# Feed-forward of the first batches in single units, engines chosen per operation by a table, and shifted ranks in a planned kernel

## The chip, the core and the metric

The kernel runs on one core of a Trainium2 chip. The core has a matrix engine (TensorE, in the profile PE, its weight loads PEld), three engines for element-wise work (VectorE or DVE, ScalarE or ACT, GpSimd or POOL), and SyncE (SP), which here only issues DMAs. Each engine runs its own list of instructions in order; they wait for each other through semaphores. Matrix products land in PSUM, of which there are eight banks of 128 x 512 float32; POOL is used in this kernel for data in SBUF only. The metric is the device time of one execution in microseconds, the median of several; less is better.

## What is computed

A recurrent state (40 x 40 per head, 4 batches x 8 heads, 768 time steps) is read and updated at each step, and its outputs pass through a feed-forward layer with a squared ReLU:

```python
for t in range(S):                         # S = 768
    y[:, :, t] = np.einsum('bhd,bhde->bhe', rt, state)
    Sa = np.einsum('bhde,bhe->bhd', state, at)
    state_decay = state * wt[:, :, None, :] - np.einsum('bhd,bhe->bhde', Sa, bt)
    state = state_decay + np.einsum('bhd,bhe->bhde', vt, kt)
...
x = y.transpose(0, 2, 1, 3).reshape(B * S, H * D)   # 3072 x 320
h = x @ w_in                                        # 320 x 2048
g = np.maximum(h, 0.0) ** 2
out = g @ w_out                                     # 2048 x 320
```

## The kernel before

Time is cut into six chunks of 128. Within a chunk the recurrence is solved with matrix products, so a chunk needs from the one before only the state at its boundary. One unit of input is a *batch* `m`: one chunk of one batch entry, all eight heads, 24 units in all (`m = 4 * chunk + entry`). Each batch is worked off in two *steps* of four heads, 48 in all (`st = 2 * m + u`).

**Preparation of a batch** (`add_prep`): SP loads six arrays of 160 KB (`W K B A V R`, L244). ACT takes the logarithm of `W` (L257), PE makes the prefix sum over time in float32 (`cs`, L263), ACT the two exponentials `GI` and `GA` (L268). `K` and `B` are multiplied by `GI` (`kb`, L279), `A`, `V`, `R` are cast to bfloat16 and `V` a second time into `EVX` (`cast`, L285 and L290). PE transposes in three groups of eight (`tGA`, `tKB`, `tRV`, all L294), and the results are copied out of PSUM as `GT` (ACT, L330), `AT` (DVE, L336), `KBT` (ACT, L342) and `RVT` (DVE, L347).

**A step** (`add_step`): eight products (`ca`, L394), masked by DVE into `CN` (L402, two operations), the triangular system solved by `P` (L411, L417), a copy `Mc` (L529), two corrections (`corr`, L426) with the difference `c1` between them (L439), and the result `Sn` (L536). `x1` (L443), `Cc` (L447) and the squares `jk`, `jm` (L451, L576) serve a check of the numbers at the end. Then `Sn` is transposed (`tb`, L463, with the state of four steps earlier, L469) and copied out (`TB`, L474), eight products `ex` (L482) are masked into `EVX` (L487, two DVE operations), and `kbm` (L498) with `z` (L505) gives the outputs and the next state, scaled on DVE into `YS` (L511) and `UZ` (L515).

**Feed-forward** (`add_ff`) is done for two batches at a time, twelve groups `h`. It waits for the `YS` of four steps. Rows of heads 6 and 7 are moved to free partitions by four small DMAs on SP (`mv`, L628). Eight groups `hp` of six products (256 columns each, L638) each fill a bank; ACT takes the ReLU (`hs`, L644), and POOL or DVE squares it (`Gt`, L649). Two halves `op` of eight products each per batch (L666) give the output, which ACT copies (`osb`, L670) and SP stores (L675). The weights come in by DMAs issued on POOL (`WIN`, L602; `WOUT`, L609).

**What sets the order.** Every operation is declared by `op(...)` with an engine, a rank (its due place, in steps), a cost, a latency, what it needs and which buffers it uses. `listed()` then plays the engines against each other in a model: at each turn it takes, for the engine that can start first, the lowest rank among the first 60 operations that could begin about then. Buffers come from rings (`RING`), PSUM banks from a pool of eight. The order in which operations are picked is the order in which they are issued, each engine in its own list. `share` puts empty operations on SP's list of the model, which stand for the time that the weights take from the DMA queues. `LATE` delays the moves and the stores in the model so that SP is not held by them.

Of the kernel before, what the change touches and what calls it, by code (L numbers as in the profile page):

```python
# [18 lines left out]
def kernel(  # L19
# [12 lines left out]
    nc = tc.nc  # L32
# [40 lines left out]
    class Op:  # L73
        __slots__ = ("name", "eng", "rank", "cost", "lat", "needs", "bufs", "mode", "fn", "end",
                     "order")
# [11 lines left out]
    def op(name, eng, rank, cost, lat, needs, bufs, fn, mode=None):  # L87
        o = Op()
        o.name, o.eng, o.rank, o.cost, o.lat, o.mode = name, eng, rank, cost, lat, mode
        o.needs, o.bufs, o.fn, o.end, o.order = list(needs), list(bufs), fn, None, len(ops)  # L90
        for b_ in o.bufs:
            b_.users.append(o)
        assert name not in ops, name
        ops[name] = o
# [24 lines left out]
    def pe(n):  # L119
        return n, n + 0.165  # L120

# [91 lines left out]

    class Batch:
# [23 lines left out]
    def add_load(m, key, rank):  # L238
# [8 lines left out]
        op(("L", m, key), "SP", rank, 0.97, 2.9, [], [o.nat[key]], go)  # L247

    def add_prep(m):
# [26 lines left out]
        def kb(u, key, j0, n):  # L276
            h = slice(2 * j0, 2 * j0 + 2 * n)
            eng = nc.vector if (m < 2 and key == "B") else nc.gpsimd
            eng.tensor_tensor(out=o.KB.tile[:, u, h, 0:D], in0=o.nat[key].tile[:, h],  # L279
                              in1=o.GI.tile[:, h], op=ALU.mult)  # L280

        def cast(key, j0, n):
            h = slice(2 * j0, 2 * j0 + 2 * n)
            if key == "X":
                nc.gpsimd.tensor_copy(  # L285
                    out=o.EVX.tile[:, j0:j0 + n, :, L:LV].rearrange("p i s e -> p (i s) e"),
                    in_=o.nat["V"].tile[:, h])
            else:
                pad = {"A": o.GA.tile[:, 1], "R": o.RV.tile[:, 0], "V": o.RV.tile[:, 1]}[key]
                nc.gpsimd.tensor_copy(out=pad[:, h, 0:D], in_=o.nat[key].tile[:, h])  # L290
# [5 lines left out]
        for p, (j0, n) in enumerate(o.parts):  # L296
# [6 lines left out]
            for u, key in enumerate("KB"):  # L303
                on = "DVE" if (m < 2 and key == "B") else "POOL"
                cost = 0.55 * f + 0.04 if on == "DVE" else 0.8 * f + 0.03
                op(("kb", m, key, p), on, sp - 2.2 + 0.1 * u, cost, cost + 0.07,
                   [("L", m, key), ("GI", m)] + cleared("KB", m), [o.nat[key], o.GI, o.KB],
                   lambda u=u, key=key, j0=j0, n=n: kb(u, key, j0, n))
            for x, (key, ring) in enumerate((("A", "GA"), ("V", "RV"), ("R", "RV"), ("X", "EVX"))):
# [4 lines left out]
                   lambda key=key, j0=j0, n=n: cast(key, j0, n))  # L314
# [14 lines left out]
            def e_gt(b1=b1, j0=j0, n=n):  # L329
                nc.scalar.activation(  # L330
                    out=o.GT.tile[:, j0:j0 + n, 1:L + 1], func=ACTF.Copy,
# [8 lines left out]
            def e_kb(b2=b2, j0=j0, n=n):  # L340
                t_ = sb(o.KBT, [128, 2, PB, L], BF16)
                nc.scalar.activation(  # L342
                    out=t_[:, :, j0:j0 + n], func=ACTF.Copy,
                    in_=bank(b2)[:, 0:2 * n * L].rearrange("p (u j t) -> p u j t", u=2, t=L))

            def e_rv(b3=b3, j0=j0, n=n):
                nc.vector.tensor_copy(  # L347
                    out=o.RVT.tile[:, :, j0:j0 + n, 0:L],
                    in_=bank(b3)[:, 0:2 * n * L].rearrange("p (u j t) -> p u j t", u=2, t=L))
# [3 lines left out]
            op(("GT", m, p), "ACT", sp - 1.8, *act(512 * f), [("tGA", m, p)] + cleared("GT", m),  # L353
               [b1, o.GT], e_gt)
# [3 lines left out]
               [o.KB, b2], t_kb, "F")  # L358
            op(("KBT", m, p), "ACT", sp - 1.1, *act(1000 * f), [("tKB", m, p)], [b2, o.KBT], e_kb)
            op(("tRV", m, p), "PE", sp - 0.6, *pe(0.45 * f),  # L360
               [("cast", m, "V", p), ("cast", m, "R", p)], [o.RV, b3], t_rv, "F")
            op(("RVT", m, p), "DVE", sp - 0.4, 0.065 + 0.535 * f, 0.145 + 0.535 * f,
               [("tRV", m, p)] + cleared("RVT", m), [b3, o.RVT], e_rv)


# [10 lines left out]
    def add_step(st):  # L376
# [65 lines left out]
        def x1():  # L442
            nc.gpsimd.tensor_tensor(out=sb(x1b[st], [128, 4, D], FP32)[:], in0=M(),  # L443
                                    in1=c1b[st].tile[:], op=ALU.add)

        def cc():
            nc.gpsimd.tensor_tensor(out=C(), in0=x1b[st].tile[:], in1=Sn(), op=ALU.add)  # L447
# [24 lines left out]
        def tb_ev():  # L472
            hi = 4 if carry else 2
            nc.vector.tensor_copy(out=sb(TB_, [128, 4, 128], BF16)[:, 0:hi], in_=tbv()[:, 0:hi])  # L474
# [46 lines left out]
        for s in range(2):  # L521
# [7 lines left out]
           lambda: nc.scalar.activation(out=M(), func=ACTF.Copy, in_=Pv()))  # L529
# [6 lines left out]
           lambda: nc.scalar.activation(out=Sn(), in_=Pv(), func=ACTF.Copy, scale=-1.0))  # L536
# [3 lines left out]
        op(("Cc", st), "POOL", st + 1.0, 0.43, 0.487, [("x1", st), ("Sn", st)],  # L540
           [x1b[st], o.EVX, Ccb[c]], cc)
# [4 lines left out]
        op(("TB", st), "DVE", st + 2.2, 0.065 + 0.00052 * n, 0.146 + 0.00052 * n, [("tb", st)],  # L546
           [tbb, TB_], tb_ev)
# [43 lines left out]
    def share(name, issue, n, each):  # L591
        for i in range(n):
            last = i == n - 1
            op(name if last else (*name, i), "SP", -5.0, each, each + 2.0 * last,
               [(*name, i - 1) if i else issue], [], lambda: None)

    def add_weights():
        for g in range(NG):
# [6 lines left out]
            op(("WINi", g), "POOL", 0.5 + 0.5 * g, 0.52 * n, 0.52 * n, [("WIN2",), GATE[g]], [], go)  # L605
            share(("WIN", g), ("WINi", g), n, 0.7)
# [3 lines left out]
        op(("WOUTi",), "POOL", 2.5, 1.23, 1.3, [GATE[3]], [], go)  # L610
        share(("WOUT",), ("WOUTi",), 9, 0.92)
        op(("WIN2",), "DVE", -5.0, 1.0, 1.1, [], [], lambda: nc.vector.memset(WIN[2][:], 0.0))

    Gtb = [buf("Gt") for _ in range(NH)]

    def add_ff(h):
        c, hf = divmod(h, 2)
        st0 = c * NQ + hf * (NQ // 2)
        done = [("YS", st0 + i) for i in range(NQ // 2)]
        X_ = YSb[c]  # L620

        def by_pair():
            return X_.tile[:].rearrange("e (b p) t -> e p b t", b=NB)[:, :, HB * hf:HB * hf + HB, :]
# [332 lines left out]
```

## Time and profile before

| what | value |
|---|---|
| time, median of three runs | 294.0 us (293.79 to 295.83) |
| the profiled execution | 294.21 us, its span 292.5 us |
| mean granted clock of TensorE | 0.967 |
| instructions | 9938 |
| data read and written in HBM | 28.84 and 3.93 MB |

The profile is of one execution. Its span is what the trace covers, 1.7 us less than that execution's time. Busy time is the union of an engine's instructions; the instructions of one engine overlap at their ends, so two that follow each other start closer together than the mean duration of one. The chain of waits, followed back from the last instruction, lies on PE for most of its length:

```profile
## 4 chain that ended last, share of the span: by engine, by line
PE 72%; DVE 9%; POOL 7%; ACT 6%; issue 2%; DMA 1%; POOLq 0%; DVEq 0%; ACTq 0%
```

Ends and starts that are used below: PE's first prefix sum starts at 4.43 us, its last product ends at 286.6 us; the last `osb` starts at 286.60 us.

### The profile page before, as it was taken

To read this page: it belongs to the slowest core of one execution; us is meant where nothing else is said; L and a number is where in the kernel's file an instruction comes from. 1 tells how busy PE (TensorE), PEld (TensorE's weight loads), DVE (VectorE), ACT (ScalarE), POOL (GpSimd) and SP (SyncE) were. 2 spreads that over 40 slices of the span, in tenths; PEclk is the share of its full clock that TensorE was granted. 3 is DMA by queue.
4 is the path that set the end of the run, shared out by engine and by line. 5 is a ranking of instruction groups with operands and counts; after the bars stand their busy time and mean duration, and the time that the engine had idled before them with its cause. 6 is when DMAs were issued, how large, how long until landed. Compare 5 with 4: busy or idle time off the path is not lost.

```text
span 292.5 us, 9938 instructions
## 1 busy us (share of the span) xinstructions
PE 272.7 (93%) x3852; PEld 216.1 (74%) x3852; DVE 227.7 (78%) x523; ACT 201.2 (69%) x531; POOL 202.9 (69%) x350
## 2 busy tenths in 40 slices
PE   6897879799998999999999999999999999999991
PEld 4665647487776788878788888888888888777871
DVE  7869988537699999999987987987987887771120
ACT  3657565387978689687687696796695776644641
POOL 7799654659998849887867878868868556555400
PEclk9959789799999999999999999999999999999998
DMA  7999794599999596978959958920010010001111
GB/s 135 180 175 183 122 174 80 102 175 180 170 173 165 101 175 120 163 136 139 192 98 178 172 101 152 145 53 25 2 31 22 2 31 25 10 23 33 44 48 53
DMA packets 158472, 31.37 MB, mean 107 GB/s; under 512 B 152976, under 2 KB 158096, under 8 KB 158416
## 3 DMA queue, kind: packets, MB, share of 16 engines
q1 hardware_dynamic: 155808, 28.03, 53.8%
q0 software_dynamic: 2608, 2.62, 5.7%
q8 instruction: 32, 0.52, 0.8%
q14 instruction: 24, 0.20, 0.2%
HBM read 28.84 MB, written 3.93 MB: 112 GB/s over the span
## 4 chain that ended last, share of the span: by engine, by line
PE 72%; DVE 9%; POOL 7%; ACT 6%; issue 2%; DMA 1%; POOLq 0%; DVEq 0%; ACTq 0%
PE bank L638 20%; PE bank L666 17%; PE bank L294 9%; PE bank L498 5%; PE bank L263 4%; PE bank L394 4%; PE bank L426 3%; PE bank L482 3%; DVE EVX L487 3%; DVE CN L402 3%; PE bank L505 2%; POOL KB L279 2%; PE bank L463 2%; ACT jk L451 2%; PE bank L469 1%
## 5 line engine op out<-in xcount | busy, mean ns | idle before, releaser
L649 POOL TENSOR_TENSOR Gt<-hs 128x512 bf16<-128x512 bf16 x66 | 68.6, 1043 | 23.0 <-ACT hs L644 22.0
L638 PE MATMUL bank<-YS,WIN 120*128 120x256 bf16 (+1 forms) x576 | 77.0, 273 | 0.0
L487 DVE TENSOR_TENSOR EVX<-bank,MEX 128x512 bf16<-128x512 f32 x96 | 64.9, 683 | 11.4 <-PE bank L482 9.2
L644 ACT ACTIVATE hs<-bank 128x512 bf16<-128x512 f32 x96 | 57.5, 601 | 22.5 <-PE bank L638 20.0
L402 DVE TENSOR_TENSOR CN<-bank,MCN 128x512 bf16<-128x512 f32 x96 | 64.5, 679 | 1.1 <-PE bank L394 1.1
L666 PE MATMUL bank<-WOUT,Gt 128*128 128x320 bf16 x384 | 60.2, 301 | 0.3 <-ACT GA L268 0.2
L638 PEld LDWEIGHTS <-WIN 120*128 120x128 bf16 (+1 forms) x576 | 51.8, 97 | 9.9 <-issue 0.6
L451 ACT ACTIVATE jk<-CN 128x512 bf16<-128x512 bf16 x48 | 30.3, 631 | 23.5 <-DVE CN L402 23.4
L666 PEld LDWEIGHTS <-Gt 128*128 128x128 bf16 x384 | 36.0, 98 | 13.5 <-issue 0.5
L443 POOL TENSOR_TENSOR x<-Mc,c 128x160 f32<-128x160 bf16 x48 | 23.5, 490 | 22.5 <-DVE c L439 21.9
L342 ACT ACTIVATE KBT<-bank 128x1024 bf16<-128x1024 bf16 (+1 forms) x25 | 24.7, 988 | 6.9 <-PE bank L294 6.8
L649 DVE TENSOR_TENSOR Gt<-hs 128x512 bf16<-128x512 bf16 x30 | 14.2, 473 | 19.6 <-ACT hs L644 19.3
L426 PEld LDWEIGHTS <-CN 128*128 128x128 bf16 x384 | 21.5, 98 | 10.3 <-issue 4.9
L279 POOL TENSOR_TENSOR KB<-NK,GI 128x320 bf16<-128x320 f32 (+1 forms) x25 | 21.2, 846 | 9.6 <-ACT GI L268 9.1
L447 POOL TENSOR_TENSOR Cc<-x,EVX 128x160 bf16<-128x160 f32 x48 | 23.7, 493 | 5.7 <-ACT EVX L536 4.9
L498 PE MATMUL bank<-EVX,KB 128*64 128x168 bf16 x384 | 23.7, 243 | 1.6 <-DVE EVX L487 1.6
L474 DVE COPY TB<-bank 128x512 bf16<-128x512 bf16 (+1 forms) x48 | 18.6, 393 | 3.7 <-PE bank L469 1.8
L511 DVE TENSOR_TENSOR YS<-bank,GT 128x256 bf16<-128x256 f32 x48 | 20.2, 420 | 1.1 <-PE bank L505 0.6
L439 DVE TENSOR_TENSOR c<-bank,Mc 128x160 bf16<-128x160 f32 x48 | 15.1, 317 | 7.3 <-PE bank L426 7.1
L394 PE MATMUL bank<-AT,KBT 64*128 64x128 bf16 x384 | 19.6, 226 | 1.2 <-DVE AT L336 1.1
L515 DVE TENSOR_TENSOR UZ<-bank,GT 64x80 bf16<-64x80 f32 x80 | 18.8, 235 | 1.9 <-PE bank L498 0.8
L263 PE MATMUL bank<-lnW,UTI 128*128 128x320 f32 x48 | 19.6, 491 | 0.8 <-DVE EVX L487 0.4
(82 smaller groups left out, 535.1 us busy)
## 6 DMA issues: line engine op xcount, KB each, us to landing
NW<-in_w_dram SPq DMA_DIRECT2D x24, 160.0 KB
NK<-in_k_dram SPq DMA_DIRECT2D x24, 160.0 KB
NB<-in_b_dram SPq DMA_DIRECT2D x24, 160.0 KB
NA<-in_a_dram SPq DMA_DIRECT2D x24, 160.0 KB
NV<-in_v_dram SPq DMA_DIRECT2D x24, 160.0 KB
NR<-in_r_dram SPq DMA_DIRECT2D x24, 160.0 KB
out_dram<-osb SPq DMA_DIRECT2D x24, 160.0 KB
WOUT<-in_moe_w_out_dram POOLq DMA_DIRECT2D x1, 1280.0 KB, 10.6
```

Of the source, the lines that this page charges most:

```text
L263: nc.tensor.matmul(out=csb.tile[:, 0:NHH * D], lhsT=UTI[:], rhs=o.lnW.tile[:], start=True, stop=True)
L279: eng.tensor_tensor(out=o.KB.tile[:, u, h, 0:D], in0=o.nat[key].tile[:, h], in1=o.GI.tile[:, h], op=ALU.mult)
L394: nc.tensor.matmul(out=quads(ca[s])[:, i, u, :], lhsT=o.KBT.tile[half(s), u, j0 + i, :], rhs=o.AT.tile[half(s), j0 + i, :], start=(i == 0 ...
L402: nc.vector.tensor_tensor(out=t_[:, :, s], in0=quads(ca[s]), in1=MCN[:], op=ALU.mult)
L426: nc.tensor.matmul(out=P[:, 2 * i + s], lhsT=CN[:, i, s, 1, :], rhs=X[:, 2 * i + s], start=False, stop=last, skip_group_check=True)
L451: nc.scalar.activation(out=t_[:], in_=CN_.tile[:, :, :, 1, :], func=ACTF.Square, accum_out=ACC[:, AN + st:AN + st + 1])
L487: nc.vector.tensor_tensor(out=EVX[:, :, s, 0:2 * LV].rearrange("p i (u x) -> p i u x", u=2)[:, :, :, 0:L], in0=quads(ex[s]), op=ALU.mult, ...
L498: nc.tensor.matmul(out=uy()[half(s), i, :], lhsT=o.KB.tile[:, u, 2 * (j0 + i) + s, :], rhs=EVX[:, i, s, LV * u:LV * u + LV], start=(i == 0 ...
L638: nc.tensor.matmul(out=hp[:, u], lhsT=WIN[g][0:ROWS[g], j * 128:(j + 1) * 128], rhs=by_pair()[0:ROWS[g], g], start=(g == 0 and u == 0), st ...
L644: nc.scalar.activation(out=sb(hsb, [128, 512], BF16)[:], in_=hpb.tile[:], func=ACTF.Relu)
L649: eng.tensor_tensor(out=t_[:, 2 * jj:2 * jj + 2].rearrange("p j a b -> p (j a b)"), in0=hsb.tile[:], in1=hsb.tile[:], op=ALU.mult)
L666: nc.tensor.matmul(out=opb.tile[:, 0:DM], lhsT=Gtb[h].tile[:, j, b_, :], rhs=WOUT[:, j, :], start=(j == 0), stop=(j == NJ - 1))
```

## The change

1. The feed-forward of batches 0 to 3 is done for one batch at a time, in groups of twelve products of 128 columns; from batch 4 on it stays with pairs. There are fourteen groups `h` instead of twelve. Their ranks follow the last step of the unit.
2. Many operations get a list of other engines on which they could run (`alts`): `kb` POOL or DVE, `cast` POOL, DVE or ACT, `GT`, `KBT`, `RVT`, `TB`, `Mc`, `Sn`, `hs` and `osb` ACT or DVE, `x1` and `Cc` POOL or DVE, the squares `Gt` any of the three. A string of digits, `WAYS`, names the one taken for each.
3. A second string, `MOVES`, shifts the rank of every operation, in tenths of a step.
4. The model has two DMA queues (`h` for those issued on SP, `s` for POOL) in place of the empty operations of `share`, and PE is 1.4 times slower in it before 56 us. The transposes name the buffers into which their results are copied, so that the plan reserves these earlier.

```diff
-    def op(name, eng, rank, cost, lat, needs, bufs, fn, mode=None):
+    def op(name, eng, rank, cost, lat, needs, bufs, fn, mode=None, alts=()):
+        o.alts = [(eng, cost, lat), *alts] if alts else []
+        o.fn = (lambda: fn(o.eng)) if alts else fn
...
+    def copy(eng, out, in_, scale=None):
+        if eng == "ACT":
+            nc.scalar.activation(out=out, in_=in_, func=ACTF.Copy,
+                                 **({} if scale is None else {"scale": scale}))
+        elif scale is None:
+            (nc.gpsimd if eng == "POOL" else nc.vector).tensor_copy(out=out, in_=in_)
+        else:
+            nc.vector.tensor_scalar(out=out, in0=in_, scalar1=scale, scalar2=None, op0=ALU.mult)
+    def engine(eng):
+        return nc.gpsimd if eng == "POOL" else nc.vector
...
-        op(("L", m, key), "SP", rank, 0.97, 2.9, [], [o.nat[key]], go)
+        op(("L", m, key), "SP", rank, 0.78, 0.78, [], [o.nat[key]], go)
+        ops["L", m, key].dma = "h", 0.85
...
-                   lambda key=key, j0=j0, n=n: cast(key, j0, n))
+                   lambda eng, key=key, j0=j0, n=n: cast(key, j0, n, eng),
+                   alts=[("DVE", *vec(320 * f)), ("ACT", *act(320 * f))])
...
-               [o.GA, b1], t_ga, "F")
+               [o.GA, b1, o.GT, o.AT], t_ga, "F")
...
-        op(("x1", st), "POOL", st + 0.9, 0.43, 0.487, [("c1", st)], [Mcb[c], c1b[st], x1b[st]], x1)
+        op(("x1", st), "POOL", st + 0.9, 0.43, 0.487, [("c1", st)], [Mcb[c], c1b[st], x1b[st]], x1,
+           alts=[("DVE", *vec(160))])
...
-    Gtb = [buf("Gt") for _ in range(NH)]
+    FFS = [(0,), (1,), (2,), (3,)] + [(m, m + 1) for m in range(4, NBC, 2)]
+    Gtb = [buf("Gt") for _ in FFS]
     def add_ff(h):
-        c, hf = divmod(h, 2)
-        st0 = c * NQ + hf * (NQ // 2)
-        done = [("YS", st0 + i) for i in range(NQ // 2)]
+        ms = FFS[h]
+        c, b0 = divmod(ms[0], NB)
+        nb, last = len(ms), 2 * ms[-1] + 1
+        NU = 4 // nb
+        done = [("YS", 2 * m + i) for m in ms for i in range(2)]
...
-            op(("mv", h, x), "SP", st0 - 9.0 + 0.01 * x, 0.82, 2.0, done, [X_], gather)
-        for jj in range(NJ // 2):
+            op(("mv", h, x), "SP", last - 12.0 + 0.01 * x, 0.75, 0.75, done, [X_], gather)
+            ops["mv", h, x].dma = "h", 0.1
+        for jj in range(NJ // NU):
...
-                hp = hpb.tile[:].rearrange("p (u a b) -> p u a b", u=2, a=HB)
-                for u in range(2):
-                    j = 2 * jj + u
+                hp = hpb.tile[:].rearrange("p (u a b) -> p u a b", u=NU, a=nb)
+                for u in range(NU):
+                    j = NU * jj + u
...
-            rank = st0 + 12.0 + 0.45 * jj
-            on = "POOL" if jj % 4 and h < NH - 1 else "DVE"
+            rank = last + 9.0 + 0.225 * NU * jj
+            ways = [("POOL", 0.99, 1.05), ("DVE", 0.34, 0.45), ("ACT", *act(512))]
...
+    COLD = 56.0, 1.4
...
-            free[e] = t + o.cost
-            o.end = t + o.lat
+            slow = COLD[1] if e == "PE" and t < COLD[0] else 1.0
+            free[e] = t + o.cost * slow
+            o.end = t + o.lat + o.cost * (slow - 1.0)
+            if o.dma:
+                kind, work = o.dma
+                begin = max(dq[kind], t + 0.4)
+                if kind == "h":
+                    over = max(0.0, dq["s"] - begin)
+                    shared = min(work, over / 2)
+                    dq["s"] += shared
+                    dq["h"] = begin + work + shared
+                    free[e] = max(free[e], dq["h"] - 2.0)
+                else:
+                    dq["s"] = begin + work + min(work, max(0.0, dq["h"] - begin))
+                o.end = max(o.end, dq[kind]) + 1.6
...
+    for o, x in zip(ops.values(), MOVES, strict=True):
+        o.rank += (SIGNS.index(x) - 45) / 10.0
+    for o, x in zip([o for o in ops.values() if o.alts], WAYS, strict=True):
+        o.eng, o.cost, o.lat = o.alts[int(x)]
     plan = listed()
```

`MOVES` has one sign for each operation of the plan, `WAYS` one digit for each operation with alternatives. The diff is cut; the other operations named in point 2 get their `alts` in the same form.

More of the change, by code (lines that the diff above doesn't have):

```diff
@@ L589 @@
     GATE = [("cast", 1, "A", 0), ("cast", 2, "A", 0), ("cast", 2, "X", 0), ("cast", 3, "A", 0)]
[L591 to L595, printed above, removed]
     def add_weights():
@@ new lines, in square @@
+            def square(eng, jj=jj, hsb=hsb):
+                t_ = sb(Gtb[h], [128, NJ, HB, L], BF16)[:, NU * jj:NU * jj + NU, 0:nb]
+                x_ = hsb.tile[:].rearrange("p (u a b) -> p u a b", u=NU, a=nb)
+                if eng == "ACT":
+                    nc.scalar.activation(out=t_, in_=x_, func=ACTF.Square)
+                else:
+                    engine(eng).tensor_tensor(out=t_, in0=x_, in1=x_, op=ALU.mult)
+            rank = last + 9.0 + 0.225 * NU * jj
+            ways = [("POOL", 0.99, 1.05), ("DVE", 0.34, 0.45), ("ACT", *act(512))]
@@ L661, in add_ff @@
-        for b_ in range(HB):
+            op(("hs", h, jj), "ACT", rank + 0.3, *act(500), [("hp", h, jj)], [hpb, hsb], relu,
+               alts=[("DVE", *vec(512))])
+            op(("Gt", h, jj), ways[0][0], rank + 0.6, *ways[0][1:], [("hs", h, jj)], [hsb, Gtb[h]],
+               square, alts=ways[1:])
+        for b_ in range(nb):
             opb, osbb = buf("bank", "ff"), buf("osb")
```

178 lines of the change are left out of this document (109 added, 69 removed).

## The prediction, made before the changed kernel was run

> **What bounds the kernel now.** I read the busy shares and the forty slices first, then a window table cut where the second and the last step write `YS` (L511 starts at 30.93 and 264.08 us), then the DMA issues on SP, then the costly groups.
>
> ```profile
> PE 272.7 (93%) x3852; PEld 216.1 (74%) x3852; DVE 227.7 (78%) x523; ACT 201.2 (69%) x531; POOL 202.9 (69%) x350
> ...
> PE   6897879799998999999999999999999999999991
> ...
> DVE  7869988537699999999987987987987887771120
> ...
> POOL 7799654659998849887867878868868556555400
> PEclk9959789799999999999999999999999999999998
> ```
>
> PE is full from the ninth slice (58 us) to the end and not before; in those first slices its granted clock dips too (5, 7, 8, 7), and DVE is at 9 while PE is not.
>
> ```profile
> core 0: us, PE busy (x) PEld busy (x) DVE busy (x) ACT busy (x) POOL busy (x), PEclk, DMA share, GB/s
> 0.00:30.93 30.93, 24.11 (x279) 17.55 (x279) 25.07 (x59) 18.15 (x53) 25.70 (x71) 0.89 1.01 170
> 30.93:264.08 233.15, 226.10 (x3392) 180.94 (x3393) 197.97 (x455) 170.86 (x457) 171.12 (x274) 0.98 0.61 106
> 90.00:140.00 50.00, 49.41 (x814) 39.65 (x812) 48.96 (x115) 40.95 (x114) 39.84 (x69) 1.00 0.82 142
> 264.00:292.50 28.50, 22.56 (x184) 17.65 (x182) 4.67 (x11) 12.19 (x22) 6.07 (x6) 0.96 0.14 46
> ```
>
> Columns: window, length, busy time of each engine with its instruction count, clock, DMA share, GB/s. From 90 to 140 us DVE (48.96) and PE (49.41 of 50) are full together. After 264 us PE alone works.
>
> **The full pace.** The prefix-sum matmul (L263) of batch 17 starts at 162.67 us, that of batch 23 at 226.47: 10.63 us per batch at clock 1.00 and with PE idle for under 0.03 in 10 us. 24 batches at this pace are 255.2 us, less 2.6 for matmuls that the first or last eight steps lack (two L505 0.14, two L411 0.07, four L469 0.11 per step). PE works from 4.43 to 286.6, 282.1 us, so 29.5 us are lost. By 60.74 (L263 of batch 5) PE had finished work worth some 32 us at this pace (four batches without feed-forward, the preparation of the fifth, nine of the L638 groups at 0.67, two of the L666 groups at 1.09) in 56.3: 24 of the loss lie there. The other 5 come mostly where DVE is full: from 80 to 90 us DVE is busy 9.81 and PE 8.44.
>
> ```profile
> 30.78 1.67 SPq L244 DMA_DIRECT2D NB<-in_b_dram  x1
> 37.03 3.31 SPq L628 DMA_DIRECT2D YS<-YS  x4
> ...
> 42.17 2.84 SPq L244 DMA_DIRECT2D NR<-in_r_dram  x1
> 50.11 3.07 SPq L628 DMA_DIRECT2D YS<-YS  x4
> 53.28 0.52 SPq L244 DMA_DIRECT2D NW<-in_w_dram  x1
> ```
>
> The start of that loss is on SP: the moves of `YS` (L628) wait on SP in their place, first till 37.03 and again till 50.11, and the loads of batches 4 and 5 stand behind them. POOL then waits 3.0 us for `NA`, and DVE falls to 4.43 busy of 10 between 50 and 60.
>
> ```profile
> L487 DVE TENSOR_TENSOR EVX<-bank,MEX 128x512 bf16<-128x512 f32 x96 | 64.9, 683 | 11.4 <-PE bank L482 9.2 <-ACT hs L644 0.8 <-ACT Mc L529 0.7
> ...
> L443 POOL TENSOR_TENSOR x<-Mc,c 128x160 f32<-128x160 bf16 x48 | 23.5, 490 | 22.5 <-DVE c L439 21.9 <-DMA NV<-in_v_dram 0.7
> ...
> L439 DVE TENSOR_TENSOR c<-bank,Mc 128x160 bf16<-128x160 f32 x48 | 15.1, 317 | 7.3 <-PE bank L426 7.1
> ...
> L649 DVE TENSOR_TENSOR Gt<-hs 128x512 bf16<-128x512 bf16 x30 | 14.2, 473 | 19.6 <-ACT hs L644 19.3
> ...
> L279 DVE TENSOR_TENSOR KB<-NB,GI 128x160 bf16<-128x160 f32 (+1 forms) x3 | 1.9, 659 | 0.8 <-ACT GI L268 0.8
> ```
>
> **Part 1, single batches.** Feed-forward of batches 0 to 3 takes 192 matmuls of 128 columns (L638) in place of 96 of 256; all other PE work has the same count. Six of 256 take 0.67 us start to start (66.74 to 67.41). Eight transposes of 128 columns (L294) take 0.55, 69 ns each, so twelve would be 0.83: +0.16 a group, +2.6 us for 16 groups; if 128 columns take half the time of 256 they cost 0. I take 2.6; it lies ahead of the last `YS`, where DVE's work (228 of 232 us, below) covers it, so it enters the sum only if PE sets the pace (A).
> The Trainium skill ("TensorE: Matmul & The Clock Gate", Back-to-back issue gap) gives some 81 ns at 128 columns; by it an estimated +4.9 us, against this cut. The row at 69 ns is less, and decides.
> The moves then need one batch's `YS`, not two. Step 1 writes it at 30.93, SP reaches that place after 28 loads at about 32 (the 27th is issued at 30.78 now), so the wait before 37.03 goes; the second set waits for step 3 (36.58 now) instead of step 7 (49.66). The loads of batch 5 move from 53 to about 40. Next late is DVE.
>
> **Part 2, engines.** Counted in the two built programs, times start-to-start spacing in the dense DVE stretch 20 to 32 us. DVE gains 30 `hs` at 0.60 (as L487, same shape) 18.0; 10 `KBT` at 0.60 (as L347) 6.0; 16 `Sn` and 4 `Mc` at 0.24 (as L439) 4.8; 34 `x1`/`Cc` at 0.29, 9.9; six `KB` at 0.65, 3.9; `GT` 1.5; seven `osb` at 0.40, 2.8; 17 casts. A cast on DVE has no row: 0.25 (scaled from L187, 256 columns in 0.21) to 0.41 (column rate of L487); I take the nearer in kind, one source in SBUF, 0.25: 4.3. Sum 51.2. It loses 14 `RVT` 8.1, 25 `TB` 7.6, seven `Gt` 2.5: 18.2. Net +33.0, of which 2.8 lie behind the last `YS` (eight `hs`, three `osb` and three squares in place of ten squares). So the stretch from step 1's `YS` to the last has 197.97 + 30.2 = 228.2 us of DVE work.
> ACT takes on 33 squares and 25 `TB` at 0.49, 38 casts at 0.41 and 14 `RVT` at 0.92, +57, and gives up 34: some 224 us of 286, not the bound. POOL gives up 26 squares (1.0 each), the 34 `x1`/`Cc` (0.43), 56 casts (0.41) and six `KB` (0.82), 68 in all: 135, off the path.
> The 0.05 in `x1`/`Cc` is the excess of the 30 squares on DVE (473 ns mean, 426 median): two sources in SBUF beside a busy POOL. It could be more, see the second rival.
>
> **Part 3, order.** Up to step 1's `YS` DVE has as much work as before (25.07). It sat idle 3.18 us between 10 and 20 while POOL issued the weights' DMAs (L602 2.26 and 2.09) ahead of batch 2's `KB` (19.51). Now `KB` of batch 2 stands ahead of `Cc`, and casts of batch 1 are on ACT and DVE. Bounds: 0 (another wait takes over) to 5.9 (all idle time before 30.93). I take 2.9: `YS` of step 1 at 28.0.
> The new cost numbers and the DMA model issue nothing themselves; the extra buffers named for the transposes reserve slots in the plan. Cost 0, their effect is in the order counted here. The last moves: two L666 groups and six L638 groups, 6.2 us, lie between the last L505 and the first group that needs them; `YS` 0.8, four issues 3.1 to 4.3, landing some 1.7 (first `NW` load, 2.97 less its issue, and less data): −0.6 to +2.0, I take 0.5.
>
> **Sum.** DVE density: 0.979 in 90:140, 0.993 from 20 to 30; I take 0.985. 228.2/0.985 = 231.7; last `YS` at 28.0 + 231.7 = 259.7 (264.1 before). Behind it PE has 14 groups at 0.665 and 10 at 1.09, 20.2 (22.6 before), + 0.5: 280.4. From PE's end to the end of the span 5.9 as now: 286.3, against 292.5. The profiled execution takes 294.21, 1.7 more than its span, and is 0.2 above the median of 294.0: 287.8 us.
>
> **Rivals.** (A) PE paces, DVE fits beside it: 252.6 at full pace and 2.6 for the small matmuls, some 14.2 of it done by 28.0 (two steps, the preparation of three batches), 3.4 lost until feed-forward can start near 37: PE ends at 28.0 + 241.0 + 3.4 = 272.4, which gives 280 us. For it: 90:140 shows both full. Against: DVE has 228 of work in 232.
> (B) Slower: DVE's two-source operations wait for POOL. Three `KB` on DVE took 325 to 1007 ns, the full one 0.93 start to start where POOL ran its own `KB` (0.86) beside it; 30 squares show only the 0.05. If each of the 57 `x1`, `Cc` and `Gt` on DVE waits half a POOL operation (0.43) in POOL's busy share (some 0.49), that is +12, 9 beyond what I count: 237/0.985, PE's end near 289.4, 297 us. It turns the sign from +6 us on. The Trainium skill ("SBUF — State Buffer", Who interferes with whom) states this as an exclusive lock between a DVE instruction with two SBUF inputs and a GpSimd one that reads SBUF. The squares at 70% POOL speak against its full price.
> (C) No change: two full engines in order wait for each other. At a density of 0.96 the last `YS` is at 265.7 and the time near 294. For it: the 80 to 90 us named above.
> That the tables do nothing is excluded: the counts above come from the built programs.
>
> **Chances.** Forecast (284 to 291) 0.44, A 0.18, B 0.16, C (291 to 297) 0.22. One per cent is about what a measurement here tells from no change. Faster: forecast and A, 0.62; within: C, 0.22; slower: B, 0.16. The range goes from A to B, 280 to 297, and leaves out half of A and half of B; the forecast's own is 284 to 291, casts at 0.41 giving 290.6.
>
> **What would show it.** Moves on SP without a wait near 30 and 38, loads of batch 5 near 40; DVE at 9.7 or more in every 10 us from 30 to 250; step 1's `YS` near 28, the last near 260; `hs` on DVE near 680 ns, casts there near 330, `x1` near 370. Wrong if DVE shows holes waiting for PE, or if `x1`, `Cc` and `Gt` on DVE last 0.2 longer than that.

## The result and the profile after

| kernel | median | runs | ratio to the kernel before, 95% interval |
|---|---|---|---|
| before | 294.9 us | 4 (293.79 to 296.66) | |
| changed | 308.0 us | 4 (307.05 to 308.55) | 1.0435 [1.0369, 1.0502] |

The changed kernel is 13 us slower; the forecast was 287.8, the range 280 to 297. Its profiled execution took 307.75 us with a span of 306.0, against 292.5 before. First the page: busy time by engine, then the forty slices (7.65 us each here).

```profile
PE 269.9 (88%) x3948; PEld 214.7 (70%) x3948; DVE 261.3 (85%) x607; ACT 218.9 (72%) x569; POOL 137.6 (45%) x228
...
PE   6467739889989949999999999999999999999991
...
DVE  7939958999989936999999999999999998976620
...
PEclk9959978999999978999999999999999999999999
```

The totals are near those of the forecast (DVE 261, ACT some 224, POOL 135). The work moved as counted; the time did not follow. The chain of waits followed back from the last instruction lay on PE for 72% of the span before; now it runs through DVE, SP's list and transfers as well:

```profile
PE 35%; DVE 30%; SPq 11%; DMA 9%; ACT 6%; issue 6%; POOL 2%; DVEq 0%; ACTq 0%; POOLq 0%
```

In the slices PE shows dents in the first six and again in the fifteenth (107 to 115 us), where DVE falls to 3 and the granted clock to 7. The window table, cut at step 1's `YS` (32.16 us) and the last (280.05), gives the sizes; columns as in the table of before.

```profile
32.16:280.05 247.89, 229.57 (x3526) 184.47 (x3524) 227.66 (x531) 190.51 (x497) 109.40 (x160) 0.97 0.57 100
280.05:306.00 25.95, 19.61 (x160) 15.35 (x158) 8.46 (x15) 10.42 (x20) 4.16 (x4) 0.98 0.14 45
30.00:60.00 30.00, 22.06 (x372) 17.78 (x371) 25.42 (x57) 19.74 (x54) 15.95 (x27) 0.89 1.00 157
60.00:90.00 30.00, 26.82 (x462) 21.95 (x458) 28.66 (x71) 24.36 (x68) 14.53 (x25) 1.00 0.77 135
90.00:120.00 30.00, 25.55 (x377) 20.23 (x372) 22.07 (x49) 21.60 (x62) 17.70 (x27) 0.89 0.90 154
120.00:240.00 120.00, 117.05 (x1785) 94.21 (x1783) 118.09 (x281) 100.98 (x259) 51.07 (x71) 1.00 0.50 92
```

Between the two `YS` DVE has 227.66 us of work (228.2 forecast) but takes 247.89: a density of 0.918 where 0.985 was taken. From 30 to 120 us it is 76.15 of 90, that is 0.846; from 120 to 240 it is 0.984, as forecast. So most of the missing time lies before 120 us, in holes of DVE and PE together. DVE does nothing for 13.9 us between 30 and 120, and 12.2 of these are waits for products of PE. What PE itself waited for longest, over the whole span, in us, times, and the longest:

```profile
PE bank L286 <- ACT lnW L280: 9.5, 5, 4.2
PE bank L661 <- DMA YS<-YS: 3.9, 1, 3.9
```

Neither is DVE; 9.2 us of the two rows lie between 30 and 120 us. `lnW` on ACT in its turn waits for the loads of `W` (13.0 us in seven waits), and the second is the first feed-forward product, which waits for the moves of `YS`. SP's list, start and duration of the issues, shows where loads and moves stand (L266 loads, L650 moves):

```profile
32.01 2.02 SPq L266 DMA_DIRECT2D NB<-in_b_dram  x1
34.12 3.42 SPq L650 DMA_DIRECT2D YS<-YS  x4
37.65 0.44 SPq L266 DMA_DIRECT2D NV<-in_v_dram  x1
38.14 2.25 SPq L266 DMA_DIRECT2D NK<-in_k_dram  x1
40.48 3.93 SPq L266 DMA_DIRECT2D NW<-in_w_dram  x1
...
58.59 3.97 SPq L650 DMA_DIRECT2D YS<-YS  x4
62.66 0.52 SPq L266 DMA_DIRECT2D NW<-in_w_dram  x1
63.30 3.22 SPq L650 DMA_DIRECT2D YS<-YS  x4
66.64 0.44 SPq L266 DMA_DIRECT2D NK<-in_k_dram  x1
```

Two things are to be seen. The moves no longer wait for `YS`, but the first four, issued from 34.12, are usable only at 44.87, when PE starts the product. And between 58.59 and 66.64 SP issues eight moves and a single load: 7.2 us of issue time for 40 KB, while the DMA share from 60 to 70 us is 0.39. After that the loads run at a DMA share of 0.73 to 1.01 for fifty microseconds and don't catch up: PE's longest wait for a `W`, 4.20 us, ends at 111.28.

Where is the kernel behind, and by when? The eighteenth step's `YS` (step 17, counted from 0) starts at 123.74 (121.22 before), and PE had by then done some 7 us less of its work, an estimate: its matmuls are counted by line up to that start in both kernels and priced with their mean spacing from 120 to 240 us in the kernel before. So about 9.5 us of the 13.5 are lost by then. Most of the rest is lost where DVE is full: PE is busy 117.05 of 120 us from 120 to 240, 119.60 before.

### The profile page after: what moved, and what is told of

It reads as the page before. It is cut to its first block, busy times and chain, and to the rows that moved or that the text cites. A ratio compares the mean times of both kernels' runs of the same rounds, so it can differ in the third digit from the quotient of the medians.

```text
span 306.0 us, 10083 instructions
## 1 busy us (share of the span) xinstructions
PE 269.9 (88%) x3948; PEld 214.7 (70%) x3948; DVE 261.3 (85%) x607; ACT 218.9 (72%) x569; POOL 137.6 (45%) x228
## 4 chain that ended last, share of the span: by engine, by line
PE 35%; DVE 30%; SPq 11%; DMA 9%; ACT 6%; issue 6%; POOL 2%; DVEq 0%; ACTq 0%; POOLq 0%
PE bank L661 12%; SPq L266 10%; PE bank L698 9%; DVE EVX L511 7%; DVE CN L425 5%; DMA NV<-in_v_dram 3%; PE bank L316 3%; DMA NW<-in_w_dram 3%; DMA YS<-YS 3%; DVE UZ L539 2%; PE bank L522 2%; DVE YS L535 2%; DVE c L462 2%; PE bank L449 2%; DVE hs L671 2%
## 5 line engine op out<-in xcount | busy, mean ns | idle before, releaser
L661 PE MATMUL bank<-YS,WIN 120*128 120x256 bf16 (+3 forms) x672 | 77.8, 261 | 4.4 <-DMA YS<-YS 3.9
L661 PEld LDWEIGHTS <-WIN 120*128 120x128 bf16 (+1 forms) x672 | 56.6, 99 | 12.3 <-issue 5.1
L698 PE MATMUL bank<-WOUT,Gt 128*128 128x320 bf16 x384 | 59.7, 302 | 0.0
L680 POOL TENSOR_TENSOR Gt<-hs 128x512 bf16<-128x512 bf16 x40 | 42.0, 1053 | 38.5 <-ACT hs L669 27.5
L669 ACT ACTIVATE hs<-bank 128x512 bf16<-128x512 f32 x66 | 38.4, 596 | 13.1 <-PE bank L661 9.8
L698 PEld LDWEIGHTS <-Gt 128*128 128x128 bf16 x384 | 36.6, 99 | 13.6 <-issue 0.5
L470 POOL TENSOR_TENSOR Cc<-x,EVX 128x160 bf16<-128x160 f32 x35 | 17.5, 500 | 41.7 <-DVE EVX L231 19.4
L449 PEld LDWEIGHTS <-CN 128*128 128x128 bf16 x384 | 20.2, 98 | 11.2 <-issue 6.6
L671 DVE TENSOR_SCALAR hs<-bank 128x512 bf16<-128x512 f32 x30 | 20.2, 681 | 7.8 <-PE bank L661 7.5
L678 ACT ACTIVATE Gt<-hs 128x512 bf16<-128x512 bf16 x33 | 20.4, 633 | 5.8 <-DVE hs L671 5.7
L466 POOL TENSOR_TENSOR x<-Mc,c 128x160 f32<-128x160 bf16 x27 | 13.4, 500 | 24.6 <-DVE c L462 24.2
L301 POOL TENSOR_TENSOR KB<-NB,GI 128x320 bf16<-128x320 f32 (+1 forms) x18 | 16.3, 906 | 11.7 <-DMA NB<-in_b_dram 6.7
L280 ACT ACTIVATE lnW<-NW 128x320 f32<-128x320 f32 x24 | 11.3, 472 | 13.0 <-DMA NW<-in_w_dram 13.0
## 6 DMA issues: line engine op xcount, KB each, us to landing
WOUT<-in_moe_w_out_dram POOLq DMA_DIRECT2D x1, 1280.0 KB, 12.9
```

Source lines behind the costliest of these rows:

```text
L301: engine(eng).tensor_tensor(out=o.KB.tile[:, u, h, 0:D], in0=o.nat[key].tile[:, h], in1=o.GI.tile[:, h], op=ALU.mult)
L449: nc.tensor.matmul(out=P[:, 2 * i + s], lhsT=CN[:, i, s, 1, :], rhs=X[:, 2 * i + s], start=False, stop=last, skip_group_check=True)
L661: nc.tensor.matmul(out=hp[:, u], lhsT=WIN[g][0:ROWS[g], j * 128:(j + 1) * 128], rhs=by_pair()[0:ROWS[g], g], start=(g == 0 and u == 0), st ...
L669: nc.scalar.activation(out=t_, in_=hpb.tile[:], func=ACTF.Relu)
L671: nc.vector.tensor_scalar(out=t_, in0=hpb.tile[:], scalar1=0.0, scalar2=None, op0=ALU.max)
L680: engine(eng).tensor_tensor(out=t_, in0=x_, in1=x_, op=ALU.mult)
```

## The experiments

Theories: **T**, in the first four runs, the transfers and the order of the plan lose the first 124 us; **T1**, the transfers of the weights take the rate from loads and moves before 60 us; **Q**, a move stands in its queue behind what was issued before it; **M**, the moves on SP keep the loads from going out; **E**, the engine table fills DVE; **S**, the small products cost PE; **O**, the shifted order itself. The kernel before ran beside each group of runs (medians 295.0 to 296.1), so ratios are compared; they are those on record and not always the quotient of the medians.

| run | median us | ratio, 95% interval |
|---|---|---|
| e7 new model alone | 298.45 | 1.006 [1.001, 1.011] |
| e4 model + single batches | 302.23 | 1.023 [1.014, 1.032] |
| e3 model + single + engine table | 306.19 | 1.038 [1.034, 1.042] |
| changed (all, shifts too) | 308.03 | 1.044 [1.037, 1.050] |
| e2 all but the engine table | 310.86 | 1.049 [1.043, 1.055] |
| e1 all, but pairs throughout | 308.64 | 1.044 [1.037, 1.052] |
| e5 changed, weights later | 308.75 | 1.046 [1.039, 1.053] |
| e6 changed, 8 moves on ACT | 317.47 | 1.071 [1.059, 1.084] |
| e8 changed, weights later, 16 moves on ACT | 311.63 | 1.053 [1.046, 1.060] |
| e13 changed, 16 moves on POOL | 302.68 | 1.025 [1.020, 1.030] |
| e14 changed, weights later, moves on POOL | 306.69 | 1.041 [1.037, 1.045] |
| e10 e4, WOUT later | 300.51 | 1.016 [1.012, 1.021] |
| e16 e4, moves on POOL | 300.71 | 1.022 [1.016, 1.027] |
| e11 e4, WOUT later, moves on POOL | 294.54 | 0.9954 [0.9923, 0.9985] |
| e15 e11 with the engine table | 299.49 | 1.017 [1.012, 1.022] |
| e9 e7, WOUT later | 300.73 | 1.013 [1.007, 1.019] |
| e17 e9, moves on POOL | 311.82 | 1.053 [1.048, 1.058] |
| e18 e11, some copies on ACT | 295.09 | 0.998 [0.994, 1.001] |
| e12 before, loads ahead of moves | 297.23 | 1.004 [1.000, 1.009] |

### The change taken apart: e1 to e4 and e7

```diff
-    FFS = [(0,), (1,), (2,), (3,)] + [(m, m + 1) for m in range(4, NBC, 2)]
+    FFS = [(m, m + 1) for m in range(0, NBC, 2)]
```

That is e1, and e7 together with neutral tables. In e2 every digit of `WAYS` is 0, in e3 every sign of `MOVES` stands for no shift, in e4 both.

> The changed kernel with the feed-forward in pairs throughout, both tables kept for every operation that has the same meaning (the first two pairs take unshifted ranks and the engines of before). Theory T (transfers and the order of the plan lose the first 124 us): the moves of step 0 and 1 no longer go out at 34 us, but the other loads still stand in the shifted order, so part of the loss goes: 298 to 305 us. Rival S (the small products of 128 columns cost PE, 16 groups by about 0.16 us): only 2.7 us come back, 305 us, and the last YS moves from 280.1 to about 277. Rival E (engine table): 306 to 309.

> The changed kernel without the engine table: every operation on its default engine, ranks still shifted, first four batches still single. Theory T: the order is what loses, so the time stays at 303 us or above. Rival E (the 33 us of extra work on DVE set the pace): DVE work falls back to about 228 us and the time to 297 us or below.

> The changed kernel without the shifts of rank: engine table kept, first four batches still single. Theory T: 10 us or more come back, 298 us or below, the prefix sum of batch 2 no longer waits for its W near 14 to 17 us, and YS of step 17 comes at 116 us or earlier (123.7 with the shifts). Rival E: DVE keeps its 261 us of work and sets the pace, so the time stays at 303 us or above and windows of 10 us show DVE at 9.7 from 30 us on.

> The changed kernel with neither table: single feed-forward of the first four batches and the new model of the transfers alone. If theory T and the single units are harmless: within 3 us of the kernel before, 291 to 297. If the loss comes from the single units or from the new model itself (rival S): 300 or above. If the engine table alone is what loses (rival E): equal to the run without the engine table.

> Neither table and feed-forward in pairs throughout: of the change only the new model of costs and transfers is left. With the single batches and no tables it took 302.2. If the single batches cost the 7 us of that run against the kernel before: within 1% of the kernel before, 292 to 298. If the new model's order of loads and moves costs them: 300 to 304, and SP's moves and loads stand in another order than before.

No single part carries the loss. In the order e7, e4, e3, changed, the steps are +0.6, +1.7, +1.5 and +0.6 per cent; the last is within the intervals. The place of e4 is loose: its four runs took 299.65, 300.12, 304.35 and 305.47 us, and by the two lower ones, one of which is the profiled one, it stands at about 1.015. Each of T, E and S failed in a run: without the engine table it was not faster (e2, against E), without the shifts 1.8 us faster, not 10 (e3, against T), with pairs not faster at all (e1, against T and S). That the time stayed at 306 or above in e1 and e3 was what E expected, and e2's time what T expected. The shifts cost 2.5 per cent or more on default engines (e2 against e4) and about nothing with the engines they stand beside. What e3 shows besides is that the 3.67 us wait for batch 2's `W` goes and that DVE is at 9.6 to 10.0 of 10 from 120 to 210 us, but for 8.98 from 140 to 150; `YS` of step 17 came at 122.1, not at 116.

S falls by the trace of the changed kernel: a single group of twelve products takes 0.85 us, and eighteen in a row 1.19, so twelve take 0.69 from start to start, against 0.67 for six of 256 columns.

### Weights later: e5, e9, e10

The finished plan is reordered, nothing else:

```diff
     plan = listed()
+    x_ = next(i for i, p in enumerate(plan) if p[1].name == ('WOUT',))
+    it_ = plan.pop(x_)
+    y_ = next(i for i, p in enumerate(plan) if p[1].name == ('Gt', 0, 0))
+    plan.insert(y_ + 1, it_)
...
```

In e5 the first transfers of `WIN` move in the same way; in e9 and e10 the place is behind batch 5's cast of `A`.

> The changed kernel, all of it, with two places in the finished plan moved: the first five transfers of WIN stand behind the K product of batch 1 (near 14.5 us, 10.1 in the changed kernel) and WOUT behind the first square (near 48 us, 31.7 in the changed kernel). Theory T1 (the weights take the transfer rate that loads and moves need before 45 us): the 3.67 us that PE waits for the logarithm of batch 2 shrink to under 1.5, the 3.87 us before the first feed-forward product to under 1, NB of batch 4 is used at 40 instead of 44.3; 5 us or more come back, 303 us or less. Rival Q (the moves stand in a queue behind loads issued before them, whatever the weights do): the wait before the first feed-forward product stays above 2.5 us; 306 or more. Rival E (DVE has too much work): the time stays within 2 us of 308, since DVE takes up what PE gains.

> Model alone, pairs throughout (298.45 us), with WOUT moved in the finished plan from 30.8 to about 56 us; its first use there is at 84 us. Theory T1 (WOUT takes the transfer rate from the loads of batches 4 and 5): the waits of PE for the products of K and B at 43 and 45 us, 4.4 and 1.8, go, the loads of batch 4 and 5 are issued at 0.6 to 1.0 us each instead of up to 4.7, and 3 us or more come back: 295.5 or less. Rival P (PE order of this plan is worse in itself): no more than 1 us comes back.

> Single batches without tables (302.2 us), WOUT moved from 30.5 to about 54 us; first use at 73. Theory T1: the 4.95 us wait for the product of B at 43 us goes, 3 us or more come back, 299 or less. If the single batches cost by their small products (rival S), the distance to the run with pairs and WOUT later stays near 3.8 us.

T1 by itself falls, and instructively. In e5 both waits named in the expectation are gone, and PE was busy 45.5 us of the first 60 instead of 41.7. Then it stood at 61.56, and the last row had been nowhere in the changed kernel:

```profile
PE bank L286 <- ACT lnW L280: 5.1, 4, 2.7
PE bank L316 <- ACT RV L226: 5.0, 1, 5.0
```

`YS` of step 17 starts at 123.74 in e5 and in the changed kernel alike: what was gained early was given back to the next load that was late. e9 repeats it (waits of 4.4 and 1.8 us for products at 43 and 45 us become one of 5.5 for a cast at 64), and e10 gains 0.7 per cent in place of the 1 or more expected, within the intervals, and nothing on e4's two lower runs. WOUT takes its 10.6 to 14.2 us of transfer wherever it stands, and one or two of the loads issued meanwhile take some 4 us of SP's time (4.25 here), where most take 0.5 to 1.0:

```profile
51.45 3.40 SPq L650 DMA_DIRECT2D YS<-YS  x4
54.95 0.52 SPq L266 DMA_DIRECT2D NV<-in_v_dram  x1
55.52 1.88 SPq L266 DMA_DIRECT2D NR<-in_r_dram  x1
57.52 4.25 SPq L266 DMA_DIRECT2D NW<-in_w_dram  x1
```

(SP's list in e10, WOUT issued at 49.55 us.) So a later place helps only where the loads are far enough ahead; e11 below is such a case.

### Moves off SP: e6, e8, e16, e11

```diff
-                nc.sync.dma_start(out=by_pair()[row:row + n, p], in_=by_pair()[src:src + n, hh // 2])
+                (nc.gpsimd if h < 4 else nc.sync).dma_start(
+                    out=by_pair()[row:row + n, p], in_=by_pair()[src:src + n, hh // 2])
```

(`nc.scalar` in e6, with `h < 2`, and in e8.)

> The changed kernel with the moves of the first two single batches (eight small transfers) issued by ACT, which has a queue of its own, at the same place of the plan. Rival Q (first in, first out behind the loads on SP's queue): the moves land 2 to 3 us after their issue instead of 8, the 3.87 us wait before the first feed-forward product goes, 3 to 4 us come back: 304 to 305. Theory T1 (the transfer rate itself): the moves still take 5 us or more to land and less than 1.5 us comes back. ACT pays some 5 us of issue time, which lies in windows where it is busy two thirds of the time.

> Both edits in one: weights later as above, and the moves of all four single batches on ACT. Theory T1 with Q (both matter): 300 us or below, YS of step 17 at 117 or earlier (123.7 in the changed kernel). If the first 124 us are not set by transfers: 305 or above.

> Single batches, no tables, WOUT where the plan puts it (30.5 us), moves of the single batches on POOL: e4 (302.2) with this one difference, e11 without WOUT later. Theory M alone: 295 to 297. If WOUT later is needed as well: 298 or above, with the wait for the product of B near 43 us (4.95 in e4) still there.

> As the run before, and the 16 moves of the single batches issued by POOL instead of SP. Theory M (the doubled moves cost SP 0.75 us each, in which no load goes out): loads of batches 5 and 6 go out 6 us earlier by 70 us, and 2 to 4 us come back against the run before. Rival S: no difference, or slower by POOL's issue time (16 of some 0.55 us) and by its wait for YS ahead of products and casts.

ACT was the wrong place: in e6 it stood 15.9 us at the first move, until 51.95, and PE 15.3 us behind it; the row names a load of `V` as releaser (of `R` in e8), and why a move should wait for that load is not settled. e8 shows the same with 9.1 us. These two say nothing on Q.

On POOL the picture is clearer. e10 and e11 differ only in which engine issues the sixteen moves, and the time falls from 1.016 to 0.995, 2.1 per cent or 6 us, more than the 2 to 4 that M expected. In e10 the sixteen moves take 12.0 us of SP's time, and SP waits 2.6 us more in front of them; how much each of the two counts, the pair doesn't tell. SP's list in e11, in the place of the four rows above:

```profile
51.95 0.70 SPq L266 DMA_DIRECT2D NV<-in_v_dram  x1
52.70 0.69 SPq L266 DMA_DIRECT2D NR<-in_r_dram  x1
53.48 0.89 SPq L266 DMA_DIRECT2D NW<-in_w_dram  x1
54.46 1.58 SPq L266 DMA_DIRECT2D NK<-in_k_dram  x1
56.16 4.79 SPq L266 DMA_DIRECT2D NB<-in_b_dram  x1
```

The loads are slowed by WOUT here as well (4.79), but by then they are a batch ahead. Counted from SP's lists:

| loads issued before | 50 us | 60 us | 70 us |
|---|---|---|---|
| before | 30 | 39 | 49 |
| changed | 35 | 43 | 48 |
| e13 | 37 | 47 | 57 |
| e10 | 39 | 43 | 48 |
| e16 | 38 | 48 | 58 |
| e11 | 45 | 51 | 57 |

In e10 PE waits 4.1 us for a cast of `A` at 61.9 us and 2.7 near 95; in e11 no wait of PE after 30 us is longer than 1.2. Neither edit does it alone: e16, with WOUT at 30.8, keeps a wait of 3.9 us for the product of `B` at 42.8 and gains 0.1 per cent on e4, nothing on its two lower runs. (The kernel before gets by with 30 loads at 50 us because its plan starts on the `op` products at 56.9 us and reaches the ninth `YS` only at 75.9; e11 needs its loads for that `YS` at 69.6.)

### Back to the changed kernel: e13, e14, and what WOUT does to a move behind it: e17

> The changed kernel, both tables, with only the 16 moves of the single batches issued by POOL instead of SP. Theory M (moves on SP keep loads from going out): loads run without a break through 58 to 67 us, the 4.2 us wait for the logarithm near 111 us goes, 4 to 7 us come back, 301 to 304. Rival O (the shifted order of the loads themselves): the wait near 111 us stays, less than 2 us come back. Either way the stretch from 120 us on stays 2.5 us looser than before, by the engine table.

> As e13 with the weights later as in e5 too. Theory M with T1: 298 to 301; the waits at 14 to 17 us (3.7), at the first feed-forward product (3.9), at 61 us (5.0 in e5) and at 111 us are all gone, and what is left above the kernel before is the engine table. Rival O: 304 or above.

> Pairs throughout, no tables, WOUT later (as e9, 300.7), and the eight moves of the first two pairs on POOL: e11 with pairs in place of the single batches. Theory M (moves on SP hold up loads): 295 to 298, and the 5.5 us wait for the cast of A at 64 us in e9 goes. If the single batches themselves gain by letting feed-forward begin earlier: 1.5 us or more above e11 (294.5), that is 296 or more; if their small products cost 2.7 us (rival S): at or below 294.

M holds in the changed kernel too: e13 gives back 1.8 per cent, 5.3 us, the wait at 111 us is gone and `YS` of step 17 starts at 119.03 (123.74). But PE waits 4.87 us at the first feed-forward product, more than before, and e14, meant to be the sum of two good edits, is worse than e13: PE waits 9.0 us for moves, 8.2 of it at 59.76. In both, moves were issued by POOL after WOUT, which goes through the same queue. In e14 the four that PE waits for landed 11.1 to 12.8 us after their issue, the last of them 1.0 us after WOUT, where the other moves of that run took 1.5 to 4.2. In e13 three took 7.7 to 10.5 and landed within 0.8 us of WOUT; the fourth, which ends PE's wait, landed in 3.1, but POOL issued it only at 43.64, behind a cast that waited 4.5 us for a load of `R`. e17 shows it bare, by chance of the place chosen for WOUT; first POOL's list, then PE's:

```profile
51.01 0.59 POOL L650 DMA_DIRECT2D YS<-YS  x1
...
52.00 1.20 POOL L628 DMA_DIRECT2D WOUT<-in_moe_w_out_dram  x1
53.19 0.53 POOL L650 DMA_DIRECT2D YS<-YS  x1
```

```profile
66.16 1.23 PE L662 MATMUL bank<-YS,WIN 120*128 120x256 bf16 x5 [11.25 <-DMA YS<-YS]
```

Three of the four moves go ahead of WOUT, the fourth behind it, 12 KB at most behind 1280 KB, and PE stands 11.25 us. The fourth lands 12.7 us after its issue, 0.2 us after WOUT; the three ahead of WOUT took 2.9 to 4.4. So Q is shown for POOL's queue (the landings of SP's moves are mostly not in the traces), and e17 can't answer what it was run for: whether the single batches gain anything once their moves are off SP stays open.

### The engine table with the transfers out of the way: e15, and a piece of it: e18

e15 is e3 with the two edits of e11. In e18 the table is neutral but for

```diff
+    for o in ops.values():
+        if o.name[0] == "TB" and 2 <= o.name[1] < 14 or o.name[0] == "RVT" and 2 <= o.name[1] < 7:
+            o.eng, o.cost, o.lat = next(x for x in o.alts if x[0] == "ACT")
```

> Engine table without shifts of rank, WOUT later and the moves on POOL: e11 (294.5) with the engine table as its only difference. Theory E (DVE with 33 us more work runs at its limit from 120 us on and costs PE some 3 us): 297 to 299. If the engine table does no harm once loads are free: 294 to 296; if it helps, as the change means it: below 294.

> e11 with one small part of the engine table's idea: the copies of the transposed products of steps 2 to 13 and of R and V of batches 2 to 6 on ACT instead of DVE (about 12 x 0.3 and 5 x 0.58, 6.5 us, off DVE; 11 us on ACT, which is busy 19.7 of 30 us there). If DVE sets the pace between 30 and 60 us in e11: 1 to 3 us faster than e11, 291.5 to 293.5. If PE or transfers set it: 294 to 296.

E holds: the table costs 2.1 per cent, some 5 us, where loads are free, as expected (299.5 by the median, at the upper end of the 297 to 299). Both kernels start step 16's `YS` near 112.5 us; after that e15 falls behind by 3.6 us, and one row of each window table shows where most of it goes, e15 first, then e11:

```profile
120.00:240.00 120.00, 117.16 (x1762) 93.94 (x1761) 116.51 (x278) 99.86 (x258) 48.45 (x68) 1.00 0.45 86
```

```profile
120.00:240.00 120.00, 119.83 (x1840) 98.81 (x1839) 103.93 (x237) 91.61 (x246) 90.77 (x144) 1.00 0.46 86
```

With DVE at 104 of 120 us PE loses 0.17; with DVE at 116.5 it loses 2.84. The whole stretch between step 1's and the last `YS` in e15 has 226.14 us of DVE work in 239.38: 0.945, not 0.985, though PE never waited over 1.5 us for anything after 30 us. e18 took 5.7 us off DVE (226.66 to 220.95) and gained nothing over e11 that its interval shows; PE then waited 3.0 us for a product of `B` at 62.3, and POOL 2.2 for WOUT.

### The kernel before, with its loads first: e12

```diff
     plan = listed()
+    for m_, h_ in ((4, 0), (5, 1)):
+        late = [p for p in plan if p[1].name[0] == "mv" and p[1].name[1] == h_]
+        y_ = plan.index(late[0])
+        early = [p for p in plan[y_:] if p[1].name[:2] == ("L", m_)]
+        for p in early:
+            plan.remove(p)
+        plan[y_:y_] = early
```

> The kernel before, untouched but for SP's list: the loads of batch 4 stand ahead of the first four moves, those of batch 5 ahead of the second four, so that SP does not hold loads back while it waits for YS at 32.5 to 37.0 and 45.0 to 50.1. If transfers that stand behind waiting moves set the early loss (the reading on record): 1 to 4 us faster, 291 to 294, and POOL's 3.0 us wait for A of batch 6 shrinks. If WOUT and the loads then share the rate and the moves land late, as in the changed kernel: within 1 us of 295 or slower.

This tests the reading on which the forecast rested, and it fails: SP's list is now free of waits ahead of the loads of batches 4 and 5, and the kernel is not faster. The moves go out at 38.33 and 52.84 (37.03 and 50.11 before), the ninth `YS` at 78.89 (75.88). So the loads come earlier at the price of later moves; the run shows that these waits of SP can't be taken away for nothing, and not what else holds the early stretch back.

The fastest version found is e11: new model, single batches, no tables, WOUT later, moves on POOL. It is 0.5 per cent faster than the kernel before, an interval that excludes no change but lies within the one per cent called no change above.

## Why the prediction was wrong

**Full pace, and the 24 us lost before 60.74.** That loads behind waiting moves start this loss is not borne out: e12 takes that wait away and gains nothing. A likely reason, not shown, is that the gaps of SP (a DMA share of 0.77 from 30 to 60, 0.86 in e12) let WOUT and the moves through quickly: WOUT took 10.6 us there, 12.2 in e12 and 12.9 in the changed kernel. What does lose the 24 us stays open.

**Part 1.** "The wait before 37.03 goes", "loads of batch 5 move from 53 to about 40": so it was (34.12 without a wait, `W` of batch 5 at 40.48). The step that failed is that nothing was charged for what is moved: sixteen moves of some 0.75 us of SP issue each in place of eight, among loads that now keep the DMA engines full (a share of 1.00 from 30 to 60), and the only landing that was priced, that of the last moves, was put at some 1.7 us, where PE started some 8 us after the issue of the fourth move into that traffic. Taking the sixteen moves off SP gives 5.3 us back in the changed kernel (e13) and 6 in e11 against e10; in e16 against e4 it gives nothing, as PE still waits 3.9 us near 43. "Next late is DVE" was false: next late were the loads. The 2.6 us for small products were too much by the trace (0.02 a group, 0.3 in all); the Trainium skill's figure ("TensorE: Matmul & The Clock Gate", Back-to-back issue gap) is further off, since 0.69 us for twelve is 57 ns each.

**Part 2.** Right: 227.66 us of DVE work against 228.2; `hs` on DVE 681 ns (near 680). Most casts took 328 to 546 ns by form (near 330 told), `x1` 410 (near 370) and `Cc` 516.

**Part 3.** Step 1's `YS` was forecast at 28.0 with bounds of 0 to 5.9 gained; it came outside them, at 32.16, 1.2 later than before. PE stood 3.67 us at batch 2's prefix sum for `W`, because `WIN`'s first transfers go out at 10.05 instead of 14.64 us; in e5, where they don't, that wait is gone. Moving POOL's list was priced, the transfers that it issues were not.

**Sum.** Span 286.3 forecast, 306.0 measured: 4.2 at step 1's `YS`, 16.2 in the stretch (247.9 against 231.7), −0.7 in the tail (25.95 against 26.6, as told). The mis-sized term is the density. Holes from 30 to 120 us make 13.9 of the 20.2 us in which DVE does nothing; the forecast had 3.5 for all. In that stretch DVE waits 12.2 us for products of PE and PE 9.2 for `W` and moves; "wrong if DVE shows holes waiting for PE" was the right test. And e15 shows that 0.985 was too high even without them: 0.945, near rival C's 0.96. The 0.979 came from 50 us in which nothing was late, and the changed kernel reaches 0.984 from 120 to 240 us; it is the whole stretch that does not keep it.

**Rivals.** B had the sign but not the mechanism: DVE's total was as forecast, so no lock added 9 us to it; `Cc` at 516 ns here and 401 in e15 leaves open a small share (13 times 0.115, 1.5 us). A would need PE at full pace from 37 us on; it was busy 74.4 of the 90 us from 30 to 120. C's loose pair of full engines is real and worth some 5 us (e15 against e11), in place of costing only the gain. The rival that happened, transfers late in an in-order list, was not among them, although DMA shares near 1.00 until 30 us and WOUT's 10.6 us stood in the profile of before.

**Still open:** of the 13 us, e13 ties 5.3 to the moves on SP and e15 some 5 to the engine table, in a plan of another order; the rest is not taken apart. Open too are how much the shifts cost by themselves (the intervals of e3 and the changed kernel overlap), and the single batches with free moves.

## What to carry to other kernels

When a change removes a wait in front of a transfer, ask what the transfer now runs beside: count issues on the issuing engine and what stands ahead in its queue, as instructions are counted. A density read from 50 us in which two full engines run well is a best case, not the mean of the 230 us that follow a change. A wait that goes is only a gain if the next load is early enough; count loads issued by a given time before and after.

## What the runs showed of the hardware that was not expected

- On POOL's queue a small transfer behind a large one waits for it: behind WOUT's 1280 KB PE stood 8.2 and 11.25 us for moves of at most 12 KB (e14, e17), while moves on POOL's queue in e11 and e16 landed in 3.2 to 3.5 us (median). In e11 too the four moves behind WOUT took 8.3 to 10.7 us, but PE had other work. The Trainium skill ("DMA: Bandwidth & Descriptors", Queues, rings and completion order) has each DMA engine turn between queues packet by packet, and, where it tells of the queues of SP and ACT, take each ring in order; these rows show that order for POOL's queue, and say nothing on the turns.
- While WOUT is being transferred, the issue of one or two loads on SP takes some 4 to 6 us (e10 4.25, e11 4.79 and 4.21, e15 3.91 and 5.78); the median of the other loads is 0.7. That SP's queue is then full is a guess.
- A stall can cost twice. In the changed kernel the granted clock was 0.66 from 110 to 120 us, around PE's wait of 4.20 us, with PE busy 8.54 of 10: eight products of L698 took 2.34 us at 112.92 and 1.25 at 105.20. A stall is not needed for a lower clock: it was 0.83 from 30 to 60 us in the kernel before, where no gap between PE's products was over 1.2 us.
